# Gated FNet and attention mix: the last 22 units with whole products, two projection chains sooner, and maxima turned one section later

## The chip, the cores and the metric

The kernel runs on one core of a Trainium2 chip. The metric is the device time of one execution in microseconds (us). The times of before are three runs; one further execution was profiled, and the page and the trace come from it.

## The reference

The input x has 2048 rows of 512 columns. Two branches are mixed by a gate that is computed from x, one number for each row.

```
def _A_ref(x, dft_seq_re, dft_seq_im, dft_hid_re, dft_hid_im):
    a = einsum("bsd,ed->bse", x, dft_hid_re)
    b = einsum("bsd,ed->bse", x, dft_hid_im)
    return einsum("ts,bse->bte", dft_seq_re, a) - einsum("ts,bse->bte", dft_seq_im, b)

def _B_ref(x, wqkv, wo):            # H = 32 heads of 16 columns, S = 2048
    qkv = (x @ wqkv) ...            # split into q, k, v by head
    p = softmax(q @ k.T * 16 ** -0.5)
    return (p @ v, heads side by side) @ wo

g = sigmoid((x * gate_w).sum(-1, keepdims=True))
return g * _A_ref(...) + (1 - g) * _B_ref(...)
```

Everything is float32. The kernel keeps that accuracy by splitting a matrix into a high part and a remainder, and by taking three products (high-high, high-remainder, remainder-high) for one.

## The kernel before

The work has three stages. In the first (up to line 276) q, k, v and the transform along the hidden axis are computed with whole matmuls (128 rows of the array). In the second, the attention of 32 heads runs together with the transform along the sequence. In the third, the attention's output is divided by its sums, projected with `wo`, gated and written.

**Units.** Heads are taken in pairs; head 0 of a pair uses rows 0 to 63 of the TensorE array and head 1 rows 64 to 127, so that two matmuls of half height run at the same time. A pair has 32 units, and 16 pairs make 512 units. A unit is one block of 128 keys against 1024 queries (half `hf` of the queries). `scores(u, qb, h)` (line 554) makes a block of 128 x 512 scores in a bank of `psS` (three banks) and ScalarE takes the exponential of it into the tile `pt`; a unit has four such blocks. `pv(u)` (line 566) multiplies the four blocks with v, on four column groups of the array, into the bank `acc` ("the values of a unit"). After the sixteenth unit of a half `acc` is copied and stored.

**Maxima.** Softmax needs the largest score of each query ahead of time. `a_tile(i, h)` (line 196) computes a block of scores the other way round into a bank of `psA` (three banks), and VectorE takes the maximum along it into `mx`. Whenever the 64 blocks of one pair and half are done, VectorE reduces them to `nm`, and `(p, hf)` goes into the list `deferred`. `m_rows(p, hf)` (line 211) turns these maxima with a transpose on TensorE, copies them with two VectorE operations, and SyncE (SP) issues four DMAs that put them into two rows of `qs`; the scores of that pair and half take them in by their matmul (50 rows instead of 48). The maxima run ahead of the scores by `LEAD` blocks for each head, which are made in stage 1 among the whole matmuls (line 253).

**Products.** Next to the scores TensorE has a second stream of matmuls: first those of the sequence transform (`dft`, 32 chains of 48 products), then the projections (`proj(hf, cts, pools)`, chains of three products for each of the column tiles `cts`). A `Chain` accumulates in one bank (`psD`, or `psA` where `pools` names it). A product has 128 rows. In a section it is issued as two halves of 64 rows, one in each of two consecutive segments, so that a half product on one half of the array stands beside a score or a maxima block on the other half.

**Order.** TensorE, VectorE, ScalarE and SP each work through one queue in the order in which the program issues; the order is written by hand. A `segment` (line 712) handles two units and follows a pattern: a small letter is a slot with a half product and a score (`s`) or maxima (`a`) block of the other head; two letters are a slot with a block of each head; `|` stands for the values of one unit. FULL has 16 slots and 16 products, THIN 14 slots and up to 12 products. The two halves of a product must not accumulate into the bank at the same time. So the first product of a segment waits for the engine that used the last block of the segment before (`last_user`, line 725). At the end of a segment `run_deferred` issues the transposes of maxima that came due.

From unit 482 on the loop at the end (line 766) uses `weave` instead: nine products a section, first their halves on rows 64 to 127 and then their halves on rows 0 to 63, beside the scores of the two heads, with a TensorE drain (`turn`) ahead of each half; then the values of two units. Sections still have maxima blocks until unit 490. `start` sets which projection fills the sections. `plan` and `at(u, ...)` say ahead of which unit the other steps are issued: `sums` and `inverse` (the reciprocals of the softmax sums by way of DRAM), `block` and `last_block` (loading, multiplying and splitting the attention's output), `load_yg` and `load_w15`. `last_pair` (line 494) finishes the last head pair after the last values.

Of the kernel before, what the change touches and what calls it, by code (L numbers as in the profile page):

```python
# [9 lines left out]
F32 = mybir.dt.float32  # L10
# [5 lines left out]
P = 128  # L16
# [5 lines left out]
KT = D // P  # L22
NT = S // P
UNITS = NP * 32
LEAD = 42
RAW = 6
PSUM = bass.MemoryType.PSUM
DRAM = bass.MemoryType.DRAM
# [3 lines left out]
def mix_kernel(ctx: ExitStack, tc: tile.TileContext, xa_t, xa, wqkv, w_hid, w_seq, wo, gate_w, out):  # L32
# [191 lines left out]
    def run_deferred():  # L224
        while deferred:
            m_rows(*deferred.pop(0))
# [14 lines left out]
    for s in range(NT):  # L241
        ab[s] = t = xab[s // 4][:, s % 4]
        if s + 2 < NT:
            xgs[s + 2] = staged(xa[s + 2])
        xg = xgs.pop(s)
        pss = []
        for c in range(3):
            ps = psS.tile([P, 512], F32, name="s")
            pss.append(ps)
            for kt in range(KT):  # L250
                k = slice(kt * P, (kt + 1) * P)
                mm3(ps, t[:, 0, k], t[:, 1, k], wch[:, c, kt], wcl[:, c, kt], kt == 0, kt == KT - 1)
            for _ in range(2 if c == 1 and s % 4 == 0 else 1):
                if s >= 3 and a_next < LEAD:
                    a_tile(a_next, 0)
                    a_tile(a_next, 1)
                    a_next += 1
                    if a_next % 32 >= 4:
                        run_deferred()
            if c == 0:  # L260
                pv = ps.rearrange("p (r h d) -> p r h d", h=2, d=DH)
                nc.scalar.copy(vt[:, s, :, 0:16], pv[:, :, 0])
                nc.vector.tensor_copy(vt[:, s, :, 17:33], pv[:, :, 1])
        hi_lo(t[:, 0], t[:, 1], pss[1])
# [286 lines left out]

    pts = {}

    def scores(u, qb, h):
        p, r = divmod(u, 32)
        hf, kt = divmod(r, 16)
        q0 = hf * 1024 + qb * 512
        if u not in pts:
            pts[u] = work.tile([P, 4, 512], F32, name="pt", bufs=4)
        spare = a_next >= NP * 64 and qb and u < 500  # L560
        ps = psA.tile([P, 512], F32, name="a") if spare else psS.tile([P, 512], F32, name="s")
        rr = slice(64 * h, 64 * h + 50)
        nc.tensor.matmul(ps, ks[p % 2][rr, kt * P:(kt + 1) * P], qs[p % 2][rr, q0:q0 + 512], start=True, stop=True)  # L563
        return nc.scalar.activation(pts[u][:, 2 * qb + h], ps, AF.Exp, bias=0.0, scale=DH ** -0.5)  # L564
# [27 lines left out]

    def issue(x, half, stop=True):
        chain, st, mv, after, last = x
        i = chain.mm(st, mv, half, last and stop)
        if stop and after:
            after()
        return i

    def turn():  # L600

        nc.tensor.drain()

    def pump(gen, n):
        for x in take(gen, n):
            issue(x, None)

    def drain(gen):
        while xs := take(gen, 9):
            for x in xs:  # L610
                issue(x, None)

    def weave(q, ds):

        m = len(q[0]) - 1
        n = min(len(ds), m)
        if ds:
            turn()
        for i in range(n):
            q[0][i]()  # L620
            issue(ds[i], 1, False)
        for x in ds[n:]:
            issue(x, 1, False)
        for i in range(n, m + 1):
            q[0][i]()
            q[1][i - n]()
        rest = q[1][m + 1 - n:]
        if ds:
            turn()
        for i, x in enumerate(ds):  # L630
            issue(x, 0)
            if i < len(rest):
                rest[i]()

    fill = iter(())
    plan = {2: [gate]}

    def at(u, f, *args):
        plan.setdefault(u, []).append(partial(f, *args))
# [9 lines left out]
                    for step, du in enumerate((16, 20, 22)):  # L649
                        at(last + du + 8 * half, block, step, hf, ct, half)  # L650

    def start(gen, n, whole=True):
        nonlocal fill, rate
        drain(fill)
        fill, rate = gen, (n, whole)

    one, more = [(psD, "d")], [(psD, "d"), (psA, "a"), (psA, "a")]
    at(482, start, proj(0, (0, 1, 2), one), 9)
    at(482, load_yg, 0, range(8))
    for step, u in enumerate((490, 494, 496)):  # L660
        at(u, last_block, step, 1, 3, nc.gpsimd)
    at(500, start, proj(1, (3,), more), 9, False)
    for step, u in enumerate((500, 502, 504)):
        at(u, last_block, step, 0, 4, nc.vector)
    at(506, start, proj(0, (3,), more), 9, False)
    at(500, load_w15)
    rate = (7, True)
    lead = a_next

    def ahead(k):  # L670
        return min(lead + 4 * k, NP * 64)

    def queue(k, h):

        q = []
        for i in range(4):
            q.append(partial(scores, 2 * k + i // 2, i % 2, h))
            if ahead(k) + i < NP * 64:
                q.append(partial(a_tile, ahead(k) + i, h))
        return q  # L680

    def run_plan(k):
        for f in plan.get(2 * k, []) + plan.get(2 * k + 1, []):
            f()
        if k % 16 == 0 and k // 16 + 1 < NP:
            load_stacks(k // 16 + 1)

# [2 lines left out]

    FULL = "a s a s a s s a s a s a s a s a | |"
    THIN = "aS s s a a s a | a s a a s s sA |"

    def stream(h):

# [4 lines left out]

    streams = [stream(h) for h in range(2)]

    def score(kind, h):
        x = next(streams[h][kind == "a"], None)
        if x:
            last_user[0] = (a_tile if kind == "a" else scores)(*x)

    last_user = [None]  # L710

    def segment(k, pattern, half, ds, stop):

        before = last_user[0]
        ds = iter(ds)
        u = 2 * k
        for slot in pattern.split():
            if slot == "|":
                pv(u)
                u += 1  # L720
                continue
            if len(slot) == 1:
                x = next(ds, None)
                i = x and issue(x, half, stop)
                if i and before is not None:
                    tc.add_manual_dep(
                        i.ins, before.ins.name,
                        mybir.DependencyInfo(mybir.DependencyClass.Sync, mybir.DependencyReason.DATA))
                    before = None
            score(slot[0], 1 - half)  # L730
            if len(slot) == 2:
                score(slot[1].lower(), half)
        run_deferred()

    def pairs():

        seq = dft()
        for i in range(2 * NT):
            for _ in range(4 if i % 2 else 3):
                yield THIN if i % 2 else FULL, take(seq, 12 if i % 2 else 16)  # L740
        seq = proj(1, (0, 1, 2), one)
        for i in range(8):
            yield THIN, take(seq, 9)

    run_plan(0)
    for i in range(4):
        for kind in "sa":
            for h in range(2):
                score(kind, h)
    pv(0)  # L750
    pv(1)
    for i in range(4):
        score("s", 0)
        score("a", 0)
    last_user[0] = None
    k = 1
    for pattern, ds in pairs():
        for half in range(2):
            run_plan(k)
            a_next = ahead(k)  # L760
            segment(k, pattern, half, ds, half == 1)
            k += 1
    for f in queue(k, 1):
        f()
    a_next = ahead(k + 1)
    for k in range(k, UNITS // 2):
        run_plan(k)
        if 2 * k in pts:
            continue
        q = [queue(k, 0), queue(k, 1)]  # L770
        a_next = ahead(k)
        weave(q, take(fill, *rate))
        pv(2 * k - 2)
        pv(2 * k - 1)
        run_deferred()
    pv(UNITS - 2)
    pv(UNITS - 1, evac=False)
    last_pair(fill)


# [34 lines left out]
```

## Time and profile before

| what | value |
|---|---|
| three runs, median (lowest to highest) | 1835.68 us (1835.26 to 1836.51) |
| the profiled execution, its own time | 1838.79 us |
| span of the profiled execution | 1837.0 us |
| TensorE matmul busy (PE) | 1803.5 us, 98% of the span |
| VectorE busy (DVE) | 1424.6 us, 78% |
| ScalarE busy (ACT) | 1164.2 us, 63% |
| GpSimd busy (POOL) | 306.5 us, 17% |
| mean DMA rate | 90 GB/s |

The page names engines by short names: PE is TensorE (PEld its weight loads), DVE is VectorE, ACT is ScalarE, POOL is GpSimd, SP is SyncE, which issues the DMAs. In a line of the timeline the columns are start (us from the beginning of the span), duration (us), engine, line of the kernel, operation, output tile and inputs, shapes and the number of instructions; a bracket gives the idle time ahead and what ended it. In a line of the window table the columns are the window, its length, the busy time (and instructions) of PE, PEld, DVE, ACT and POOL, the granted TensorE clock (1.00 is full), the share of the DMA engines and GB/s. The ends of matmuls are modelled; their starts are what the steps are read from.

### The profile page before, as it was taken

To read this page: it belongs to the slowest core of one execution; us is meant where nothing else is said; L and a number is where in the kernel's file an instruction comes from. 1 tells how busy PE (TensorE), PEld (TensorE's weight loads), DVE (VectorE), ACT (ScalarE), POOL (GpSimd) and SP (SyncE) were. 2 spreads that over 40 slices of the span, in tenths; PEclk is the share of its full clock that TensorE was granted. 3 is DMA by queue.
4 is the path that set the end of the run, shared out by engine and by line. 5 is a ranking of instruction groups with operands and counts; after the bars stand their busy time and mean duration, and the time that the engine had idled before them with its cause. 6 is when DMAs were issued, how large, how long until landed. Compare 5 with 4: busy or idle time off the path is not lost.

```text
span 1837.0 us, 32546 instructions
## 1 busy us (share of the span) xinstructions
PE 1803.5 (98%) x12672; PEld 1034.7 (56%) x12672; DVE 1424.6 (78%) x2375; ACT 1164.2 (63%) x2240; POOL 306.5 (17%) x317
## 2 busy tenths in 40 slices
PE   8999999999999999999999999999999999999998
PEld 7876665555555545555555555554655455544554
DVE  5236668888888888888888888888888888888824
ACT  5311126777777777767676677767676777777664
POOL 1210011111212123121112222221112221100000
PEclk9999989999999999999999999999999999999999
DMA  8783233131414153414271434223231524360212
GB/s 283 256 194 106 69 97 60 39 67 36 76 36 70 37 111 94 81 36 70 89 211 49 76 100 100 58 53 64 63 66 49 110 89 87 116 184 7 71 37 92
DMA packets 77994, 164.71 MB, mean 90 GB/s; under 512 B 14592, under 2 KB 15616, under 8 KB 74000
## 3 DMA queue, kind: packets, MB, share of 16 engines
q1 hardware_dynamic: 77584, 162.56, 35.1%
q8 instruction: 100, 1.64, 0.4%
q14 instruction: 54, 0.44, 0.1%
q0 software_dynamic: 256, 0.07, 0.0%
HBM read 107.47 MB, written 54.52 MB: 88 GB/s over the span
## 4 chain that ended last, share of the span: by engine, by line
PE 94%; DVE 4%; issue 1%; ACT 1%; DMA 0%; DVEq 0%; SPq 0%; ACTq 0%
PE d L316 34%; PE acc L572 26%; PE a L201 12%; PE s L563 8%; PE s L78 4%; PE s L79 3%; PE s L80 3%; DVE mx L203 2%; PE a L78 1%; PE a L79 1%; PE a L80 1%; PE a L316 1%; DVE yp L456 1%; DVE rc L397 0%; PE a L213 0%
## 5 line engine op out<-in xcount | busy, mean ns | idle before, releaser
L203 DVE TENSOR_REDUCE mx<-a 128x1 f32<-128x512 f32 x2048 | 1280.9, 683 | 261.3 <-PE a L201 208.9
L564 ACT ACTIVATE pt<-s 128x512 f32<-128x512 f32 x2032 | 1060.3, 612 | 447.2 <-PE s L563 385.3
L201 PE MATMUL a<-ks,qs 48*128 48x512 f32 x2048 | 809.8, 428 | 5.4 <-DVE mx L203 5.4
L563 PE MATMUL s<-qs,ks 50*128 50x512 f32 x2032 | 739.8, 418 | 3.7 <-DVE xab L75 1.8
L316 PE MATMUL d<-xab,ch 64*128 64x512 f32 x2048 | 671.5, 405 | 8.5 <-DVE mx L203 6.6
L572 PE MATMUL acc<-pt,vt 128*17 128x512 f32 x4096 | 537.6, 598 | 0.0
L316 PEld LDWEIGHTS d<-xab,ch 64*128 64x128 f32 x2048 | 358.4, 185 | 203.1 <-issue 118.1
L201 PEld LDWEIGHTS a<-ks,qs 48*128 48x128 f32 x2048 | 373.7, 186 | 160.4 <-DVE mx L203 120.9
L563 PEld LDWEIGHTS s<-qs,ks 50*128 50x128 f32 x2032 | 365.7, 186 | 73.9 <-ACT pt L564 35.2
L316 PE MATMUL d<-xab,cl 64*128 64x512 f32 x1024 | 406.0, 396 | 0.0
L295 POOL CAST ch<-craw 128x512 fp32r<-128x512 f32 x128 | 78.2, 611 | 1132.8 <-PE s L563 678.6
L316 PEld LDWEIGHTS d<-xab,cl 64*128 64x128 f32 x1024 | 189.1, 185 | 42.1 <-DVE mx L203 23.8
L572 PEld LDWEIGHTS acc<-pt,vt 128*17 128x17 f32 x4096 | 87.3, 96 | 198.4 <-issue 187.0
L296 POOL TENSOR_TENSOR cl<-craw,ch 128x512 fp32r<-128x512 f32 x128 | 164.1, 1282 | 10.2
L316 PE MATMUL d<-wo_hl,o_hl 64*128 64x512 f32 x288 | 78.7, 405 | 3.8 <-DVE mx L203 2.9
L78 PE MATMUL s<-wch,xab 128*128 128x512 f32 x192 | 79.9, 416 | 0.0
L80 PE MATMUL s<-wch,xab 128*128 128x512 f32 x192 | 76.0, 396 | 0.0
L79 PE MATMUL s<-wcl,xab 128*128 128x512 f32 x192 | 75.9, 395 | 0.0
L74 ACT CAST xab<-s 128x512 fp32r<-128x512 f32 x16 | 9.4, 585 | 97.6 <-PE s L79 97.6
L316 PEld LDWEIGHTS d<-wo_hl,o_hl 64*128 64x128 f32 x288 | 49.5, 184 | 30.2 <-issue 17.7
L78 PEld LDWEIGHTS s<-wch,xab 128*128 128x128 f32 x192 | 36.0, 188 | 16.1 <-issue 6.4
L75 DVE TENSOR_TENSOR hl<-s,hl 128x512 fp32r<-128x512 f32 x32 | 22.0, 686 | 27.1 <-ACT hl L74 27.1
(101 smaller groups left out, 693.3 us busy)
## 6 DMA issues: line engine op xcount, KB each, us to landing
craw<-w_seq SPq DMA_DIRECT2D x128, 256.0 KB
qk<-hl SPq DMA_DIRECT2D x32, 512.0 KB
qs<-qk SPq DMA_DIRECT2D x96, 128.0 KB
ks<-qk SPq DMA_DIRECT2D x96, 128.0 KB
b<-hl SPq DMA_DIRECT2D x16, 512.0 KB
xab<-b SPq DMA_DIRECT2D x16, 512.0 KB
o<-oe SPq DMA_DIRECT2D x62, 128.0 KB
oh<-nh SPq DMA_DIRECT2D x12, 512.0 KB
```

Source lines behind the costliest of these rows:

```text
L75: (lo_eng or nc.vector).tensor_tensor(lo, src, hi.bitcast(F32), ALU.subtract)
L78: nc.tensor.matmul(ps, sh, mh, start=first, stop=False)
L79: nc.tensor.matmul(ps, sh, ml, start=False, stop=False)
L80: nc.tensor.matmul(ps, sl, mh, start=False, stop=last)
L201: nc.tensor.matmul(ps, qs[p % 2][r, qt * P:(qt + 1) * P], ks[p % 2][r, kb * 512:(kb + 1) * 512], start=True, stop=True)
L203: user = nc.vector.tensor_reduce(mx[p % 2][:, h, qt, kb:kb + 1], ps, AX.X, ALU.max)
L295: nc.gpsimd.tensor_copy(h1, raw)
L296: nc.gpsimd.tensor_tensor(l1, raw, h1.bitcast(F32), ALU.subtract)
L316: i = nc.tensor.matmul(self.ps, st[r], mv[r], start=not self.begun, stop=stop)
L563: nc.tensor.matmul(ps, ks[p % 2][rr, kt * P:(kt + 1) * P], qs[p % 2][rr, q0:q0 + 512], start=True, stop=True)
L564: return nc.scalar.activation(pts[u][:, 2 * qb + h], ps, AF.Exp, bias=0.0, scale=DH ** -0.5)
L572: nc.tensor.matmul(acc[32 * j:32 * j + 17], vt[:, kt, p, 16 * h:16 * h + 17], pt[:, j], start=kt == 0, stop=kt == NT - 1)
```

## The change

- `LEAD` goes from 42 to 44: two more pairs of maxima blocks are made in stage 1, for which six instead of three insertions are doubled.
- Pairs and segments: after the eight pairs of segments with `proj(1, (0, 1, 2))` two more pairs take the first two chains of `proj(0, (0, 1, 2))`. All ten pairs use two new patterns (NINE) with 12 and 13 slots for nine products.
- Maxima are turned one segment after they are complete, behind the first values of that segment, instead of at the end of the segment in which they are complete.
- The wait of a segment's first product goes to the last `s` block behind the last product of the segment before, where there is one, instead of to the last block.
- Last 22 units (490 to 511): `weave` and its drains go. A section issues three pairs of scores (head 0 in a `psS` bank, head 1 in a `psA` bank), then nine or six products as whole matmuls of 128 rows, then the fourth pair, then the values of two units. The last twelve products are issued in `last_pair`.
- The steps of the last blocks are planned for units 488, 492, 496 (from 490, 494, 496) and 500, 504, 504 (from 500, 502, 504). The loads of the stacks go into the plan at the same units as before.

```
-LEAD = 42
+LEAD = 44
...
-            for _ in range(2 if c == 1 and s % 4 == 0 else 1):
+            for _ in range(2 if c == 1 and s % 2 == 0 else 1):
...
-    def scores(u, qb, h):
+    def scores(u, qb, h, other=False):
...
-        spare = a_next >= NP * 64 and qb and u < 500
-        ps = psA.tile([P, 512], F32, name="a") if spare else psS.tile([P, 512], F32, name="s")
+        ps = psA.tile([P, 512], F32, name="a") if other else psS.tile([P, 512], F32, name="s")
...
-    def turn():
-
-        nc.tensor.drain()
-
     def pump(gen, n):
-        for x in take(gen, n):
+        for x in take(gen, n, False):
             issue(x, None)
...
-    def weave(q, ds):
...
-    for step, u in enumerate((490, 494, 496)):
+    for step, u in enumerate((488, 492, 496)):
         at(u, last_block, step, 1, 3, nc.gpsimd)
...
-    for step, u in enumerate((500, 502, 504)):
+    for step, u in enumerate((500, 504, 504)):
         at(u, last_block, step, 0, 4, nc.vector)
...
     FULL = "a s a s a s s a s a s a s a s a | |"
     THIN = "aS s s a a s a | a s a a s s sA |"
+    NINE = "sA s s a a sA | a a s a s aS |", "aS a s s a aS | sA a s a s s sA |"
...
+    def segment(pattern, half, ds, stop):
+        nonlocal users
+        before, users = users, []
+        due, deferred[:] = deferred[:], []
         ds = iter(ds)
         for slot in pattern.split():
             if slot == "|":
-                pv(u)
-                u += 1
+                values()
+                while due:
+                    m_rows(*due.pop(0))
                 continue
             if len(slot) == 1:
                 x = next(ds, None)
+                if x:
+                    i = issue(x, half, stop)
+                    users = []
+                    if before:
+                        tc.add_manual_dep(
+                            i.ins, dict(before).get("s", before[0][1]).ins.name,
...
-        run_deferred()
...
-        seq = proj(1, (0, 1, 2), one)
-        for i in range(8):
-            yield THIN, take(seq, 9)
+        for seq, n in ((proj(1, (0, 1, 2), one), 8), (first, 2)):
+            for i in range(n):
+                yield NINE, take(seq, 9)
...
+    run_plan(valued)
+    for i in range(4):
+        score("s", 1)
+    run_deferred()
+    pump(first, 9)
+    third = proj(1, (3,), more)
+    last = proj(0, (3,), more)
+    whole = {492: (first, 9), 494: (first, 9), 496: (first, 9), 498: (first, 9), 500: (first, 9), 502: (third, 9),
+             504: (third, 9), 506: (third, 6), 508: (last, 6), 510: (last, 6)}
+    for u in range(valued + 2, UNITS, 2):
+        run_plan(u)
+        for i in range(4):
+            if i == 3:
+                pump(*whole[u])
+            for h in range(2):
+                scores(u + i // 2, i % 2, h, h == 1)
+        values()
+        values()
     pv(UNITS - 2)
     pv(UNITS - 1, evac=False)
-    last_pair(fill)
+    last_pair(last)
```

`values()` issues `pv` for the next unit in turn, and `one` and `more` are `[psD]` and `[psD, psA, psA]`, the banks that the chains take in turn.

More of the change, by code (lines that the diff above doesn't have):

```diff
@@ L611, in drain @@
                 issue(x, None)
-    def weave(q, ds):
[L615 to L635, printed above, removed]
     plan = {2: [gate]}
@@ L650, in mix_kernel, with run_plan @@
                         at(last + du + 8 * half, block, step, hf, ct, half)
[L652 to L655, printed above, removed]
+    for p in range(1, NP):
+        at(32 * (p - 1), load_stacks, p)
     one, more = [(psD, "d")], [(psD, "d"), (psA, "a"), (psA, "a")]
-    at(482, start, proj(0, (0, 1, 2), one), 9)
     at(482, load_yg, 0, range(8))
-    for step, u in enumerate((490, 494, 496)):
+    for step, u in enumerate((488, 492, 496)):
         at(u, last_block, step, 1, 3, nc.gpsimd)
-    at(500, start, proj(1, (3,), more), 9, False)
-    for step, u in enumerate((500, 502, 504)):
+    for step, u in enumerate((500, 504, 504)):
         at(u, last_block, step, 0, 4, nc.vector)
-    at(506, start, proj(0, (3,), more), 9, False)
     at(500, load_w15)
-    rate = (7, True)
     lead = a_next
[L670 to L686, printed above, removed]
+    def run_plan(u):
+        for v in sorted(v for v in plan if v <= u + 1):
+            for f in plan.pop(v):
+                f()
     FULL = "a s a s a s s a s a s a s a s a | |"
     THIN = "aS s s a a s a | a s a a s s sA |"
+    NINE = "sA s s a a sA | a a s a s aS |", "aS a s s a aS | sA a s a s s sA |"
     def stream(h):
@@ L703, in mix_kernel @@
     streams = [stream(h) for h in range(2)]
+    users, valued = [], 0
     def score(kind, h):
@@ L707, in score, with values @@
         if x:
[L708 to L714, printed above, removed]
+            users.append((kind, (a_tile if kind == "a" else scores)(*x)))
+    def values():
+        nonlocal valued
+        pv(valued)
+        valued += 1
+    def segment(pattern, half, ds, stop):
+        nonlocal users
+        before, users = users, []
+        due, deferred[:] = deferred[:], []
         ds = iter(ds)
-        u = 2 * k
         for slot in pattern.split():
             if slot == "|":
-                pv(u)
-                u += 1
+                values()
+                while due:
+                    m_rows(*due.pop(0))
                 continue
@@ L723, in segment @@
                 x = next(ds, None)
[L724 to L729, printed above, removed]
+                if x:
[4 more added lines that the diff above has]
+                            i.ins, dict(before).get("s", before[0][1]).ins.name,
+                            mybir.DependencyInfo(mybir.DependencyClass.Sync, mybir.DependencyReason.DATA))
+                        before = None
             score(slot[0], 1 - half)
@@ L739, in pairs @@
             for _ in range(4 if i % 2 else 3):
-                yield THIN if i % 2 else FULL, take(seq, 12 if i % 2 else 16)
-        seq = proj(1, (0, 1, 2), one)
-        for i in range(8):
-            yield THIN, take(seq, 9)
+                yield ((THIN,) * 2, take(seq, 12)) if i % 2 else ((FULL,) * 2, take(seq, 16))
+        for seq, n in ((proj(1, (0, 1, 2), one), 8), (first, 2)):
+            for i in range(n):
+                yield NINE, take(seq, 9)
+    first = proj(0, (0, 1, 2), one)
     run_plan(0)
@@ L749, in mix_kernel @@
                 score(kind, h)
-    pv(0)
-    pv(1)
+    values()
+    values()
     for i in range(4):
@@ L754, in mix_kernel @@
         score("a", 0)
-    last_user[0] = None
-    k = 1
-    for pattern, ds in pairs():
+    users = []
+    for patterns, ds in pairs():
         for half in range(2):
[L759 to L775, printed above, removed]
+            run_plan(valued)
+            segment(patterns[half], half, ds, half == 1)
+    run_plan(valued)
+    for i in range(4):
+        score("s", 1)
+    run_deferred()
+    assert not any(a_left.values())
+    pump(first, 9)
[10 more added lines that the diff above has]
+                scores(u + i // 2, i % 2, h, h == 1)
+        values()
+        values()
     pv(UNITS - 2)
     pv(UNITS - 1, evac=False)
-    last_pair(fill)
+    last_pair(last)
 def kernel(A_x, A_dft_seq_re, A_dft_seq_im, A_dft_hid_re, A_dft_hid_im, B_x, B_wqkv, B_wo, gate_w):
```

## The prediction

> **What bounds it now.** I read the page first: busy times and the chain that ended last.
>
> ```profile
> PE 1803.5 (98%) x12672; PEld 1034.7 (56%) x12672; DVE 1424.6 (78%) x2375; ACT 1164.2 (63%) x2240; POOL 306.5 (17%) x317
> ...
> PE 94%; DVE 4%; issue 1%; ACT 1%; DMA 0%; DVEq 0%; SPq 0%; ACTq 0%
> ```
>
> TensorE is the bound in every stage, so time is saved by taking slots off TensorE, as long as VectorE (78%) does not take over. Then the window table, cut where the order of work changes: the 16 THIN segments with nine products (units 450 to 481), the first hand-over and weave sections, the last ten weave sections, the end.
>
> ```profile
> 1624.76:1722.36 97.60, 94.67 (x662) 45.48 (x658) 86.79 (x143) 69.51 (x131) 1.84 (x2) 1.00 0.21 49
> 1722.36:1751.44 29.08, 27.65 (x193) 16.46 (x189) 23.89 (x40) 19.21 (x37) 2.39 (x1) 1.00 0.31 101
> 1751.44:1820.60 69.16, 66.64 (x411) 35.24 (x410) 18.71 (x26) 43.21 (x85) 2.53 (x2) 1.00 0.17 48
> 1820.60:1837.00 16.40, 10.72 (x65) 5.27 (x64) 8.74 (x25) 2.27 (x10) 0.00 (x0) 0.79 0.43 161
> ```
>
> A THIN segment with nine products takes 97.60/16 = 6.10 us, a weave section 6.9, and in the weave sections VectorE (18.71 of 69.16) and ScalarE (43.21) are half idle. One weave section in the timeline of TensorE:
>
> ```profile
> 1760.66 0.49 PE L563 MATMUL s<-qs,ks 50*128 50x512 f32 x1
> ...
> 1762.84 0.39 PE L563 MATMUL s<-qs,ks 50*128 50x512 f32 x1
> 1763.33 0.49 PE L316 MATMUL d<-wo_hl,o_hl 64*128 64x512 f32 x1
> ...
> 1764.12 1.55 PE L316 MATMUL d<-wo_hl,o_hl 64*128 64x512 f32 x6
> 1765.60 1.91 PE L572 MATMUL acc<-pt,vt 128*17 128x512 f32 x16
> 1767.76 0.47 PE L563 MATMUL s<-qs,ks 50*128 50x512 f32 x1 [0.25 <-issue]
> ```
>
> A slot (one matmul, or two on the two row halves) is 0.232 us: six in 1.55 with 0.39 for the last. The section is 7.1 us: 19 slots (nine half products, nine more, one pair of scores alone) = 4.4, two units of values = 1.75, the rest edges and two drains (0.49 instead of 0.23 at 1762.84).
>
> **Tail sections, units 492 to 511.** Afterwards a section has four pairs and nine whole products: 13 slots = 3.02 instead of 4.4. Two values with their edges and no drain: a FULL segment is 5.95 between values in the timeline, less 16 slots leaves 2.24. Switching from pairs to whole rows and back has a row in stage 1, where a pair stands among whole matmuls:
>
> ```profile
> 133.49 0.40 PE L80 MATMUL s<-wch,xab 128*128 128x512 f32 x1
> 133.82 0.50 PE L201 MATMUL a<-ks,qs 48*128 48x512 f32 x2
> 134.25 0.50 PE L78 MATMUL s<-wch,xab 128*128 128x512 f32 x1
> 134.58 0.40 PE L79 MATMUL s<-wcl,xab 128*128 128x512 f32 x1
> ...
> 137.24 0.73 PE L201 MATMUL a<-ks,qs 48*128 48x512 f32 x3
> 138.53 0.50 PE L201 MATMUL a<-ks,qs 48*128 48x512 f32 x1 [0.55 <-DVE mx L203]
> 138.96 0.50 PE L78 MATMUL s<-wch,xab 128*128 128x512 f32 x1
> ```
>
> From 133.49 to 134.58 are 1.09 for three slots (0.70): 0.40 for both switches. So 5.66 by this sum; walking the gaps one by one (0.52, 0.33, 0.23, 0.43, 0.34, 1.63, 0.33, 0.34, 1.32) gives 5.47. I take 5.55, and 4.85 for a section with six products. The Trainium skill, "TensorEngine Tiling (Array Packing)", Key Properties, says that a change of tiling mode drains TensorE, which speaks against mixing whole and halved matmuls; the trace agrees, at 0.40 us. With free switches the ten sections would sum to 4 us less; the page has no price.
>
> ScalarE has eight exponentials a section; a row of eight below takes 4.03, under 4.85. The sixth score bank is free when pair 3 comes, since the products stand in between. In sections 502 to 510 the products share the three psA banks with head 1's scores: a product waits for the exponential of pair 0 or 1, about 0.35 in 502 and 504, 0.1 to 0.2 later (between 0 and 1 each). In 504 the cast of the last raw block queues ahead of the exponentials on ScalarE (1.08), behind a multiply on VectorE that needs a DMA. In before that multiply started at 1789.81 and the values of unit 495 ended at 1774.4: 15.4 us. The new place is three sections later, some 16 us: cover just enough, 0.6 more taken for the cast, 2 to 4 if the DMA is late. Sum: 5 x 5.55 + 5.9 + 6.5 + 5.05 + 2 x 4.95 = 55.1. The hand-over ahead of it (four single scores, one transpose of maxima, nine whole products) is 1.6 + 0.3 + 2.4 = 4.3.
>
> **Units 450 to 489, pattern NINE.** Twelve and thirteen slots instead of fourteen: 12.5 x 0.232 = 2.90, and two separate values at 0.87 + 0.41 of edges = 2.56; 5.46. (The same sum for THIN gives 5.81; it measures 5.88 with twelve products.) With nine it measures 6.10 because the first product of the next half waits for the last maximum, which stands behind the evacuation of the chain:
>
> ```profile
> 1636.92 0.50 PE L563 MATMUL s<-qs,ks 50*128 50x512 f32 x1
> 1637.78 0.49 PE L316 MATMUL d<-wo_hl,o_hl 64*128 64x512 f32 x1 [0.36 <-DVE mx L203]
> ...
> 1733.29 4.95 DVE L203 TENSOR_REDUCE mx<-a 128x1 f32<-128x512 f32 x8 [0.96 <-PE a L201]
> ...
> 1796.70 4.03 ACT L564 ACTIVATE pt<-s 128x512 f32<-128x512 f32 x8 [1.82 <-PE d L316]
> ```
>
> That wait goes, as it is tied to an exponential (0.50 each) instead. What is late next is VectorE: per pair of segments 16 maxima at 0.62, an evacuation 0.75, 0.2 of row work = 10.87, 5.43 a segment. TensorE and VectorE are level. I take 5.55; floor 5.34, ceiling the present 6.10. Twenty segments: 111.0.
>
> From 1624.76 (0.98 behind the start of unit 449's values, where the first such segment begins) to the end of the last values (1824.05, the last pass at 1823.63 plus 0.42) are 199.3 us. Afterwards 111.0 + 4.3 + 55.1 + 1.75 = 172.2: **-27.1**.
>
> **The end.** Twelve whole products (four chains) move behind the last values. TensorE is idle there, but four evacuations at 0.66 enter VectorE's queue between the reciprocals and the last eight evacuations, and those 21% of the chain's last 22 us end last: **+2.4** (1.5 to 3).
>
> **Stage 1.** LEAD 44 needs six double insertions of maxima instead of three, and one single less. A single costs 0.64, a double 1.91 (the second pair waits for a psA bank, row 138.53): 3 x 1.27 = +3.8. The pair dropped at 257.6 no longer stands ahead of VectorE's subtraction that the second score waits for (idle 1.75 at 260.06): -1.1. **+2.7.**
>
> **The middle.** Turning maxima is moved: the transposes go one section later, behind its first values. In before each costs 0.21 and none waits for VectorE beyond the end of the values. In THIN that stays; in FULL it now splits two values: 13 times 0.25, between 0 and 0.5 (nearest: edges of 0.41 around a single value): +3.2. SP issues its four DMAs 0.9 to 2.9 us sooner; nothing queues behind them. The other change is the wait of the first product, "s" instead of the last user:
>
> ```profile
> 608.18 1.09 ACT L564 ACTIVATE pt<-s 128x512 f32<-128x512 f32 x2
> ...
> 608.82 0.47 PE L316 MATMUL d<-xab,ch 64*128 64x512 f32 x1 [0.23 <-ACT pt L564]
> ...
> 1201.41 0.47 PE L316 MATMUL d<-xab,ch 64*128 64x512 f32 x1 [0.89 <-DVE mx L203]
> ```
>
> Inside a chain both users end within 0.1 us of each other: nothing. Where a chain of the first matrix ends, ScalarE evacuates it and the exponential ends at 609.27, so the product moves from 608.82 to 609.40: 8 x 0.58 = +4.6. Where one of the second ends, VectorE evacuates and the product need not wait for the maximum: 4 x 0.65 + 3 x 0.77 = -4.9. The plan's earlier loads at 488 and 492 move on SP and POOL alone, 15 us ahead of use: nothing. **+2.9.**
>
> Sum: -27.1 + 2.4 + 2.7 + 2.9 = **-19.1**. The profiled execution took 1838.79 us (span 1837.0 and 1.8 around it), 3.1 above the median of 1835.68; taken off the median, **1816.5 us**.
>
> **Rivals.**
> VectorE takes over in NINE: three psA banks do not bridge the values, segments stay near 6.1. For: 5.43 of 5.55. Against: VectorE ran eight in a row without a gap. 20 x 0.55: 1827.5. Chance 0.15.
> The last block's DMA or the shared psA banks hold the tail: for, VectorE already waited 2.0 us for that DMA; against, 7 us of slack to its user. +4: 1820.5. Chance 0.10.
> The clock: after the 1.75 us without TensorE work at 260.06 the granted clock is 0.50 in windows of 5 us from 260 to 275 and 0.79 in the next, some 17 us; the change cuts that gap to about 1. If the clock stays, values and a segment run at full speed until VectorE's 20 maxima bind: -5.5, 1811. Against: the slots there stay 0.6 apart. Chance 0.10. The Trainium skill, "TensorE: Matmul & The Clock Gate", Why this matters for your kernels, puts the limit at idle gaps over some 3 us; by that rule not even the old gap should have cost the clock, and the trace disagrees.
> Slower: the rows of maxima reach qs too late, so that the scores of each of 30 groups wait. It decides from 19.1/30 = 0.64 us each; at 1 us, 1846.5. Against: they are issued sooner than before. Chance 0.05.
> The gain is not there, since the sections become bound by ScalarE's latency and stay near 6.9 and NINE near 6.1: 1835. Chance 0.04.
> My sum: 0.56.
>
> **Range.** 0.2% (3.7 us) is what can be told from no change. Low 1806: the VectorE floor in NINE (-4.2) and the clock rival. High 1828: the first rival. Left out are the last two. Faster 0.91, same 0.03, slower 0.06.
>
> **What would show it.** Values of one NINE segment to the next 5.4 to 5.7 apart; tail sections 5.4 to 5.7 and 4.7 to 5.0, without 0.49 gaps; at the ends of first-matrix chains the product released by an exponential about 0.6 later; VectorE without a gap longer than 1 us in the end. Wrong would be NINE over 5.9, a gap of 2 us in section 504, or scores waiting for DMA of the maxima.

## The result and the profile after

The changed kernel takes **1815.79 us** (median of 4 runs, 1815.06 to 1815.92), the kernel before 1836.10 us (median of 4, 1835.26 to 1839.22). The ratio is 0.9885, 95% interval 0.9868 to 0.9903, so it is faster by 1.0 to 1.3%. Forecast were 1816.5 us. The profiled execution took 1815.83 us, with a span of 1814.0. One of the executions below, the profiled one of best_lead44 (2349.89 us), ran at a granted clock of 0.65 throughout and is left out of that kernel's time.

The page of the changed kernel, busy times and the chain that ended last:

```profile
PE 1787.5 (99%) x12570; PEld 1020.6 (56%) x12570; DVE 1423.9 (78%) x2375; ACT 1160.5 (64%) x2240; POOL 306.5 (17%) x317
...
PE 96%; DVE 2%; ACT 1%; issue 0%; DMA 0%; POOL 0%; DVEq 0%; ACTq 0%; POOLq 0%
```

TensorE has 102 matmuls fewer and is still the bound: its part of the chain went from 94 to 96%, VectorE's from 4 to 2%. VectorE's own work is what it was.

The window table of the changed kernel: nineteen and a half NINE segments, up to the end of the values of unit 488; then the last half segment, the hand-over and section 492 up to its values; from there to the values of unit 510, which are the two values of section 492 and the nine sections 494 to 510; the end from the start of these last values. The columns are busy time of PE, PEld, DVE, ACT and POOL, then the granted clock, the DMA share and GB/s.

```profile
1624.21:1735.74 111.53, 110.74 (x802) 52.13 (x798) 104.78 (x173) 81.42 (x158) 4.23 (x3) 1.00 0.26 69
1735.74:1746.46 10.72, 10.50 (x56) 6.06 (x52) 3.90 (x8) 7.70 (x16) 0.00 (x0) 1.00 0.01 2
1746.46:1797.25 50.79, 50.00 (x307) 22.43 (x309) 15.76 (x21) 40.51 (x78) 2.55 (x2) 1.00 0.19 49
1797.25:1814.00 16.75, 11.58 (x64) 6.65 (x56) 10.42 (x28) 1.71 (x8) 0.00 (x0) 0.80 0.54 204
```

TensorE's own idle time is 0.8 us in each of the two long stretches: what is left there is the length of TensorE's list and the edges between its items. VectorE is busy for 104.78 of the 111.53 us of the NINE segments (94%; 89% before), so it is near the bound and, but for one place shown further down, not on it.

A tail section in the timeline of TensorE (start, duration, engine, line, operation):

```profile
1751.89 1.91 PE L571 MATMUL acc<-pt,vt 128*17 128x512 f32 x16
1753.73 0.49 PE L562 MATMUL s<-qs,ks 50*128 50x512 f32 x1
1754.30 0.39 PE L562 MATMUL s<-qs,ks 50*128 50x512 f32 x1
1754.63 2.33 PE L316 MATMUL d<-wo_hl,o_hl 128*128 128x512 f32 x9
1756.89 0.50 PE L562 MATMUL s<-qs,ks 50*128 50x512 f32 x1
1757.32 1.05 PE L571 MATMUL acc<-pt,vt 128*17 128x512 f32 x8
```

From values to values are 5.43 us: two values 1.84, three pairs 0.90, nine whole products 2.26 from 1754.63 to 1756.89, the last pair and the step to the values 0.43. Two pairs of changes between halves and whole rows are inside these numbers, without any wait.

Two places of a NINE segment, also from the timeline of TensorE:

```profile
1633.78 0.39 PE L316 MATMUL d<-wo_hl,o_hl 64*128 64x512 f32 x1
1634.20 0.50 PE L201 MATMUL a<-ks,qs 48*128 48x512 f32 x1
1634.63 1.05 PE L571 MATMUL acc<-pt,vt 128*17 128x512 f32 x8
...
1635.61 0.50 PE L562 MATMUL s<-qs,ks 50*128 50x512 f32 x1
1635.96 0.40 PE L316 MATMUL d<-wo_hl,o_hl 64*128 64x512 f32 x1
```

The product that opens the half (1635.96) stands 0.35 us behind the first score and carries no wait; before it stood 0.86 behind and waited 0.36 for a maximum. The slot ahead of the values (1634.20, the last letters "sA" or "aS") is 0.42 from the slot before it and 0.43 from the values.

### The profile page after: what moved, and what is told of

Read it like the earlier page. It is cut to its first block, busy times and chain, and to the rows that moved or that the text cites. A ratio compares the mean times of both kernels' runs of the same rounds, so it can differ in the third digit from the quotient of the medians.

```text
span 1814.0 us, 32329 instructions
## 1 busy us (share of the span) xinstructions
PE 1787.5 (99%) x12570; PEld 1020.6 (56%) x12570; DVE 1423.9 (78%) x2375; ACT 1160.5 (64%) x2240; POOL 306.5 (17%) x317
## 4 chain that ended last, share of the span: by engine, by line
PE 96%; DVE 2%; ACT 1%; issue 0%; DMA 0%; POOL 0%; DVEq 0%; ACTq 0%; POOLq 0%
PE d L316 34%; PE acc L571 27%; PE a L201 12%; PE s L562 9%; PE s L78 4%; PE s L79 3%; PE s L80 3%; DVE mx L203 1%; PE a L79 1%; PE a L78 1%; PE a L80 1%; ACT pt L563 1%; PE a L316 0%; PE a L213 0%; DVE y L348 0%
## 5 line engine op out<-in xcount | busy, mean ns | idle before, releaser
L563 ACT ACTIVATE pt<-s 128x512 f32<-128x512 f32 x2008 | 1046.5, 612 | 423.8 <-PE s L562 367.9
L562 PE MATMUL s<-qs,ks 50*128 50x512 f32 x2008 | 730.1, 418 | 1.1 <-DVE xab L75 0.7
L201 PEld LDWEIGHTS a<-ks,qs 48*128 48x128 f32 x2048 | 369.9, 185 | 168.6 <-DVE mx L203 134.8
L562 PEld LDWEIGHTS s<-qs,ks 50*128 50x128 f32 x2008 | 359.8, 185 | 87.1 <-ACT pt L563 46.0
L316 PE MATMUL d<-wo_hl,o_hl 64*128 64x512 f32 (+1 forms) x234 | 63.2, 398 | 0.0
L316 PEld LDWEIGHTS d<-wo_hl,o_hl 64*128 64x128 f32 (+1 forms) x234 | 42.1, 186 | 13.0 <-issue 7.9
```

The source lines that it names most:

```text
L201: nc.tensor.matmul(ps, qs[p % 2][r, qt * P:(qt + 1) * P], ks[p % 2][r, kb * 512:(kb + 1) * 512], start=True, stop=True)
L316: i = nc.tensor.matmul(self.ps, st[r], mv[r], start=not self.begun, stop=stop)
```

## The experiments

Each edit is against the changed kernel. All times are medians of at least four runs; the kernel before ran beside them on the same chip, with 1837.82, 1837.32 and 1836.32 us in the three groups. The groups ran on three different chips, and the changed kernel itself beside the last of them only (the control), so a difference of 1 to 2 us to its 1815.79 is not told apart by the times; there the segments and sections in the traces decide. By "middle" are meant the stretches from the values of unit 2 to those of 252 (first matrix: 748.6 us before, 752.6 after) and from 252 to 450 (600.5 and 594.7).

**Control: the changed kernel again.**

> The changed kernel itself, unedited, beside the two on the same chip: 1815 to 1816.5; its half clock after stage 1 lasts anything from 3.4 to 17 us, in whole steps of 3.4.

Measured: 1814.86 us (1814.50 to 1815.02), ratio 0.9882 (0.9867 to 0.9897), a little under what was expected. The half clock lasts 3.4 us.

### The wait of the first product

**e1_last_user.** The product waits for the last user again, as before.

```
-  i.ins, dict(before).get("s", before[0][1]).ins.name,
+  i.ins, before[-1][1].ins.name,
```

> The changed kernel, but the first product of a segment waits again for the user of the last block of the segment before. Theory (the wait is what the first product starts on): in the middle the 8 gaps at the ends of first-matrix chains fall from 1.42 to 0.82 us and the 7 at the ends of second-matrix chains rise from 0.88 or 1.00 to 1.48 or 1.60, net about -0.6; in the ten NINE pairs the product that follows a chain's end waits about 0.5 us more, +5. Sum +4, about 1820. Rival (VectorE sets the pace of NINE by its queue, the wait does not matter): NINE stays at 5.72 us a segment, about 1815.

Measured: 1819.32 us (1816.80 to 1820.08), ratio 0.9900 (0.9885 to 0.9915). The middle moves as said: 747.8 (-4.8) and 599.3 (+4.6). In the NINE segments the wait comes back, but smaller than the 0.36 of before (timeline of this kernel):

```profile
1638.08 0.50 PE L316 MATMUL d<-wo_hl,o_hl 64*128 64x512 f32 x1 [0.16 <-DVE mx L203]
```

They take 5.87 instead of 5.72: over the twenty the kind of wait is worth 2.8 us of NINE's gain, little more than half of what was expected. That the total still came out near the 1820 expected is luck: in this execution the half clock behind stage 1 lasts 13.7 us, and the values of unit 2 start 2.0 us later (280.78 instead of 278.78). The one run with a granted clock of 0.997 took 1816.80 us.

**e2_first_user.** The product waits for the first user, whatever its kind.

```
-  i.ins, dict(before).get("s", before[0][1]).ins.name,
+  i.ins, before[0][1].ins.name,
```

> The changed kernel, but the first product of a segment waits for the user of the block that was issued beside the last product (the first in the list, not the last exponential). Theory: at the ends of first-matrix chains the exponential waited for ends 0.5 us sooner, so the 8 gaps of 1.42 fall to about 0.9, -4; the second-matrix ends stay (there the evacuation is last), NINE stays. About 1811.8. Rival (the bank's evacuation on ScalarE is what holds these products): the gaps stay at 1.42, 1815.8.

Measured: 1811.30 us (1810.46 to 1812.82), ratio 0.9860 (0.9843 to 0.9876). The first-matrix stretch takes 748.5 (-4.1); the second (594.7) and the NINE segments (5.72) stay. At the end of a chain of the first matrix the timelines show why, first in the changed kernel, then in this one:

```profile
611.07 1.08 ACT L563 ACTIVATE pt<-s 128x512 f32<-128x512 f32 x2
...
612.30 0.47 PE L316 MATMUL d<-xab,ch 64*128 64x512 f32 x1 [0.82 <-ACT pt L563]
```

```profile
609.83 0.47 PE L316 MATMUL d<-xab,ch 64*128 64x512 f32 x1 [0.33 <-ACT pt L563]
```

Behind ScalarE's evacuation stand two exponentials (x2 in 1.08 us). The changed kernel's product starts 0.15 us behind the end of the second of them, since "the score" is the last one of the list; here it starts 0.5 to 0.6 us sooner, behind the first. So the choice of "the score" gains at the chain ends of the second matrix and in NINE and loses at those of the first; "the first user" loses next to nothing there (0.33 of idle time, where before had 0.23).

### The pattern NINE and the tail sections

**e3_thin.** The NINE segments with the old pattern, but the new wait.

```
-  yield NINE, take(seq, 9)
+  yield (THIN,) * 2, take(seq, 9)
```

> The changed kernel with the pattern THIN (14 slots) in place of NINE (12 and 13) for the ten pairs with nine products. Theory A (slots set the pace): 1.5 slots of 0.232 more in each of 20 segments, less the longer edge at NINE's two-letter slots (0.09 at each value): from 5.72 to about 5.85 us a segment, +2.6, about 1818.4. Theory B (the slots alone, no edge cost): 6.07 a segment, +7, 1823. Theory C (VectorE sets the pace): no change, 1815.8.

Measured: 1820.02 us (1818.76 to 1821.28), ratio 0.9906 (0.9891 to 0.9921). A segment takes 5.94 instead of 5.72, and the twenty 4.1 us more: between what A and B expected, against C. Of the step from 6.10 to 5.72 the pattern makes 0.22, and the rest, 0.16, goes with the wait.

**e5_drains.** A drain before and behind the whole products of each tail section.

```
+  nc.tensor.drain()
   pump(*whole[u])
+  nc.tensor.drain()
```

> The changed kernel with a TensorE drain ahead of and behind the whole products of each of the ten tail sections. Theory (a switch between pairs and whole matmuls already empties the array, 0.40 us a round trip, but an explicit drain adds the restart): 0.25 us each as the drain in the middle of a weave section cost, +5, about 1820.5. Rival (the switch is a full drain by itself): no change, 1815.8.

Measured: 1818.96 us (1817.40 to 1819.52), ratio 0.9900 (0.9886 to 0.9915). The sections 494 to 500 take 5.84, +0.41; the five later ones only 0.10 to 0.17 more than without drains. In this kernel's timeline the steps into and out of the products are 0.53 and 0.58, where the changed kernel has 0.33 and 0.40:

```profile
1760.91 0.39 PE L562 MATMUL s<-qs,ks 50*128 50x512 f32 x1
1761.44 2.33 PE L316 MATMUL d<-wo_hl,o_hl 128*128 128x512 f32 x9
1763.88 0.49 PE L562 MATMUL s<-qs,ks 50*128 50x512 f32 x1
```

In these sections a drain is 0.2 us on top of a change of tiling that goes on without it.

**e6_halves.** The sections' products in halves, woven with the scores as before, with the two drains and the score banks of before; the units and the chains of the change are kept.

```
-  for i in range(4): ... pump(*whole[u]) ... scores(u + i // 2, i % 2, h, h == 1)
+  weave([[partial(scores, u + i // 2, i % 2, h, i % 2 == 1 and u < 500) ...
```

> The changed kernel with the ten tail sections issued as before: half products with two drains, no whole ones (the scores on the banks that before used). Theory (slots set the pace of the tail): seven sections with nine products have 19 slots instead of 13 (+1.39) and 0.25 more for drains, three with six have 13 instead of 10 (+0.70) and 0.25: +14 in all, sections of 7.0 and 6.0 us, about 1830. Rival (ScalarE's eight exponentials and the shared banks set the pace): under +7, sections below 6.2.

Measured: 1829.82 us (1829.06 to 1832.03), ratio 0.9964 (0.9953 to 0.9975). The sections with nine products are back at 7.0 to 7.2 us, those with six at 6.1, as the count of slots has it: 14 of the change's 20 us hang on issuing whole products, without drains. How much of the 14 goes with the drains and the score banks was not run alone; the rival (under 7 us) is out.

### Maxima turned later, and LEAD

**e4_lead42.** LEAD 42 as before, everything else as changed.

```
-LEAD = 44
+LEAD = 42
-  for _ in range(2 if c == 1 and s % 2 == 0 else 1):
+  for _ in range(2 if c == 1 and s % 4 == 0 else 1):
   ...
   score("s", 1)
+  if i < 2:
+      score("a", 1)
```

> The changed kernel with LEAD 42 and the three double insertions of before; the two blocks of head 1 that are left over come after the tenth pair, beside the single scores. Theory (what stage 1 pays for LEAD 44 is given back by the shorter stretch at half clock): the first values start 2.9 us sooner, at 265.0, the half clock lasts 17 us again instead of 6.8, the second section's values are within 1 us of the changed kernel's 278.8; +0.5 at the end; 1815 to 1816.5. Rival (the clock is a matter of chance): half clock 6.8 us again, 1813.

Measured: **1845.0 us** (1844.01 to 1846.78), ratio 1.0043 (1.0028 to 1.0058). Every theory missed it by more than 28 us. The timelines of this kernel show where they went, TensorE first, then SP's DMA queue between its second and third row:

```profile
306.27 0.28 PE L213 MATMUL a<-ident,nm 128*16 128x128 f32 x1
307.46 0.49 PE L201 MATMUL a<-ks,qs 48*128 48x512 f32 x1
310.58 0.62 PE L562 MATMUL s<-qs,ks 50*128 50x512 f32 x2 [2.63 <-DMA qs<-mt]
```

```profile
307.92 2.76 SPq L220 DMA_DIRECT2D qs<-mt  x4
```

The group of maxima is turned at 306.27, SP issues the DMAs of its four rows from 307.92 to 310.68, and the next score needs rows of its head: TensorE stands for 2.63 us. The same wait recurs, 20.6 us in 13 places. Five times the clock goes to half 0.8 to 1.6 us behind the end of one, for 3.41 us (waits of 2.63, 2.27, 1.60, 3.06 and 2.62 us); behind the other eight, of 0.27 to 1.19 us, it stays. The half clock can cost at most half of 5 x 3.41, 8.5 us, so that waits and clock together make most of the 29 us lost. In the windows of this kernel around the first the granted clock is 0.86, 0.50, 0.75 and 1.00:

```profile
310.58:312.00 1.42, 1.42 (x11) 1.37 (x12) 0.18 (x1) 0.91 (x2) 0.00 (x0) 0.86 0.03 6
312.00:314.00 2.00, 2.00 (x14) 0.48 (x11) 1.80 (x3) 1.26 (x3) 0.00 (x0) 0.50 0.00 0
314.00:316.00 2.00, 2.00 (x18) 1.01 (x12) 0.53 (x1) 0.32 (x1) 0.00 (x0) 0.75 0.00 0
316.00:318.00 2.00, 2.00 (x18) 0.63 (x14) 1.95 (x4) 1.87 (x5) 0.00 (x0) 1.00 0.00 0
```

Turning later costs the rows one section of their head start, and two more in LEAD are what buys it back. From the transpose to the first values of its group pass at least 13.9 us in before, 15.1 in the changed kernel, 13.3 in e8_lead42_end and 10.5 in this one. This is the prediction's slower rival, kept away by one constant.

**e7_rows_end.** LEAD 44, but the maxima turned at the end of the segment as before.

```
-  due, deferred[:] = deferred[:], []
   ...
-  while due:
-      m_rows(*due.pop(0))
   ...
+  run_deferred()
```

> The changed kernel (LEAD 44), but maxima are turned at the end of the segment in which they are complete, as before. Theory: in THIN and NINE they are complete with the last slot, so the transpose waits for the last maximum and its reduction on VectorE, about 0.55 us more at some 17 places, and FULL saves 0.1 at 13: +8, about 1824. Rival (the transpose needs nothing that is late): 1814.5.

Measured: 1822.32 us (1821.65 to 1823.69), ratio 0.9921 (0.9906 to 0.9936). With LEAD 44 the group is complete later in its segment, so a transpose at the segment's end comes too soon; it waits for VectorE's reduction, in 18 places and for 9.5 us in all:

```profile
347.06 0.22 DVE L207 TENSOR_REDUCE nm<-mx 128x16 f32<-128x64 f32 x1
347.33 0.28 PE L213 MATMUL a<-ident,nm 128*16 128x128 f32 x1 [0.39 <-DVE nm L207]
```

**e8_lead42_end.** Both undone: LEAD 42 and the turn at the segment's end (the edits of the last two together).

> The changed kernel with LEAD 42 (three double insertions) and the maxima turned at the end of the segment, both as before. Theory (LEAD 42 alone lost 29 us because the rows then reach qs one section too late and the scores wait for them; with the earlier turn no score waits): no stretch of half clock after the start, stage 1 is 2.9 us shorter, the middle has the six gaps of before back (+3.4): about 1815 to 1816, so that the pair of edits is worth nothing here. Rival (LEAD 42 costs by its number of blocks alone, wherever they are turned): about 1845.

Measured: 1814.30 us (1814.15 to 1816.75), ratio 0.9880 (0.9865 to 0.9894): the same as the control. The pair of edits is worth nothing; each alone loses 7 and 30 us. It is a balance of small parts: stage 1 is 3.0 us shorter (values of unit 0 at 264.85 instead of 267.89), and the middle 1.3 longer (753.1 and 595.6). For the second, the timeline of this kernel, VectorE and TensorE:

```profile
641.30 0.28 DVE L215 CAST mt<-a 16x128 fp32r<-16x128 f32 x1 [0.85 <-PE a L213]
641.61 0.28 DVE L216 TENSOR_TENSOR mt<-a,mt 16x128 fp32r<-16x128 f32 x1
641.82 1.11 DVE L397 RECIPROCAL rc<-rc 64x64 f32<-64x64 f32 x2
642.96 3.68 DVE L203 TENSOR_REDUCE mx<-a 128x1 f32<-128x512 f32 x6
643.71 0.50 PE L201 MATMUL a<-ks,qs 48*128 48x512 f32 x1 [0.39 <-DVE mx L203]
```

The copies of the maxima and two reciprocals stand in front of the next maxima, and the pair behind them finds no free psA bank. In the changed kernel the copies begin beside the second values:

```profile
641.64 1.05 PE L571 MATMUL acc<-pt,vt 128*17 128x512 f32 x8
641.75 0.28 DVE L215 CAST mt<-a 16x128 fp32r<-16x128 f32 x1
```

There the first pair of the next segment has no such wait. Before has it in six places, 0.39 to 0.63 us each, and e8_lead42_end in six again.

### A version that beats both

**best_lead44** and **best_lead42.** Three edits together, once on the changed kernel and once on e8_lead42_end (there with `s % 4`): the first-user wait; in stage 1 the second pair of maxima put into the middle of the chain, not beside the first; and the last chain on two banks in place of three, so that its products do not share psA's with the scores as often.

```
+  if kt != KT - 1 and not (kt == 1 and c == 1 and s % 2 == 0):
+      continue
-  for _ in range(2 if c == 1 and s % 2 == 0 else 1):
-  dict(before).get("s", before[0][1]).ins.name
+  before[0][1].ins.name
-  last = proj(0, (3,), more)
+  last = proj(0, (3,), more[:2])
```

> Three edits to the changed kernel together: the first product waits for the user of the block beside the last product (-4.2, measured alone); in stage 1 the six doubled insertions are pulled apart, the second pair standing in the middle of the chain, where it costs 0.64 instead of 1.27 us (-3.8); the last chains take the banks d, a in turn, so that no section begins its products on a psA bank (-0.6, section 510). If the terms add: 1807.5. Rival (what stage 1 saves is lost again at VectorE or in the half clock behind it): 1811.

> The same three edits on LEAD 42 with the maxima turned at the end of the segment: from 1814.3, -4.2 for the wait, -1.9 for three insertions pulled apart, -0.6 for the banks: 1807.6. If the six gaps of about 0.5 us, where the reciprocals stand ahead of the copies of maxima, are what LEAD 44 takes away, this one stays within 1 us of the other.

Measured: 1807.2 us (1806.28 to 1808.04), ratio 0.9840 (0.9827 to 0.9854), and 1807.35 us (1807.08 to 1808.66), ratio 0.9843 (0.9829 to 0.9856): 7.5 to 7.7 us under the control of the same group and 29 under before. The terms add up to within 1 us, and the two leads are worth the same again. The profile of best_lead42 shows the terms: the values of unit 0 start at 263.18 (264.85 in e8_lead42_end), the first-matrix stretch takes 749.1, and section 510 takes 4.98 instead of 5.59, while all other tail sections stay. Only the first of the three edits was run alone.

## Why the prediction was right, step by step

The forecast of 1816.5 us was 0.7 over the median. Its mechanism holds: TensorE's list was cut, and VectorE did not take over. Its terms were not all of the right size, and several misses offset each other: that the total is only 0.7 off is in part luck.

**From unit 450 to the end of the last values: forecast -27.1, measured -24.5** (174.8 us against 199.3). By its parts:
- *NINE*, taken at 5.55: measured 5.72 up to the values of unit 488, and 114.7 us for all twenty: 3.7 us too little. It isn't the ceiling of VectorE: the opening product carries no wait. Against the counted sum of 5.46 one edge is longer: the step from the two-letter slot to the values is 0.43, not 0.33, four times in a pair of segments, which is 0.18 a segment or a little more. And three of the ten pairs of segments are longer, 0.08 a segment on average: two in which rows are turned, by 0.4, and one, by 0.8, in which VectorE does hold TensorE up, as two reciprocals stand among the maxima (VectorE, then TensorE):

```profile
1721.18 1.12 DVE L397 RECIPROCAL rc<-rc 48x64 f32<-48x64 f32 x2
1723.07 0.49 PE L201 MATMUL a<-ks,qs 48*128 48x512 f32 x1 [0.70 <-DVE mx L203]
```

The row of 0.36 for the old wait was the right row for a wrong share: e1 gives it 0.14 a segment, e3 the pattern 0.22.
- *Sections 492 to 500*, taken at 5.55: 5.43 each from 494 on. The walk by gaps (5.47) was the better of the two sums. The hand-over ahead of them, taken at 4.3, took 3.9.
- *502 and 504*, taken at 5.9 and 6.5: 5.90 and 5.89; *506 and 508*, taken at 5.05 and 4.95: 4.98 each. The raw block's multiply came directly behind the last evacuation and waited for no DMA, and the cast hid:

```profile
1774.34 1.22 DVE L442 TENSOR_TENSOR o_raw<-o_raw 128x1024 f32<-128x1024 f32 x1
1775.58 1.05 ACT L74 CAST o_l<-o_raw 128x1024 fp32r<-128x1024 f32 x1 [0.41 <-DVE o_raw L442]
```

- *510*, taken at 4.95: 5.59. The shared psA banks, put at 0.1 to 0.2 there, cost 0.77:

```profile
1793.50 0.96 PE L316 MATMUL a<-wo_hl,o_l 128*128 128x512 f32 x3 [0.77 <-ACT pt L563]
```

**The end: forecast +2.4, measured +2.1** (16.75 us from the last values' start, 14.68 before). VectorE has the four evacuations more, as said; it now opens with one and runs through without a gap to the last:

```profile
1800.08 1.45 DVE L456 SCALAR_TENSOR_TENSOR yp_ks<-a,omg,yp_ks 128x512 f32<-128x512 f32 x2 [4.13 <-PE a L316]
...
1809.27 1.40 DVE L456 SCALAR_TENSOR_TENSOR yp<-a,omg,yp 128x512 f32<-128x512 f32 x2
```

**Stage 1: forecast +2.7, measured +2.9** at the values of unit 0, and only +0.6 at those of unit 2. The clock rival came in by half: after the shorter gaps (0.74 and 0.49 us instead of 1.75) the granted clock is 0.50 for 6.8 us, not 17.1. The windows of the changed kernel:

```profile
260.00:265.00 5.00, 3.78 (x17) 2.12 (x16) 2.91 (x7) 3.07 (x6) 0.00 (x0) 0.95 0.14 55
265.00:270.00 5.00, 5.00 (x21) 2.18 (x25) 3.91 (x7) 2.36 (x5) 1.50 (x2) 0.50 0.63 212
270.00:275.00 5.00, 5.00 (x27) 2.48 (x21) 2.79 (x6) 2.87 (x7) 4.04 (x5) 0.87 0.40 105
```

How long it stays there isn't set by the gaps: the control has the same two (0.74 and 0.49) and 3.4 us, e1 and e7 have 0.74 and 0.47 or 0.48 and 13.7 us, and e4 has one gap of 1.75, as before, and 6.8. So these 2.3 us (+2.9 at unit 0 less +0.6 at unit 2) differ between executions and can't be put down to the change.

**The middle: forecast +2.9, measured -1.7** (1347.3 against 1349.0, units 2 to 450). This is the step with the wrong sign. The two parts from the wait were right: +0.60 at each chain end of the first matrix (forecast +0.58) and -0.60 at those of the second (forecast -0.65 and -0.77); the latter in the changed kernel, where the product is released by the evacuation and not by a maximum:

```profile
1202.99 0.74 DVE L348 SCALAR_TENSOR_TENSOR y<-d,ng,yr 128x512 f32<-128x512 f32 x1
1203.88 0.47 PE L316 MATMUL d<-xab,ch 64*128 64x512 f32 x1 [0.29 <-DVE y L348]
```

Too high was the price of a turn in FULL: 0.32 between the values less 0.21 at the segment's end is 0.1, not 0.25. Not seen were the six gaps where copies and reciprocals follow each other on VectorE: 3.3 us of waits that the later turn takes away. e8, where they come back, shows it.

**How the sum stands.** The measured parts, -24.5, +2.1, +0.6 and -1.7, come to -23.5, less 0.6 that is counted twice at unit 450: the 23.0 us by which the profiled spans differ. The forecast sum was -19.1, so between the profiled executions it was 3.9 too small, 2.3 of them the clock's. The medians differ by 20.3 only, since the profiled execution of before lay 3.1 over its median of that time; the sum was taken off the median, and that is why the total came out closer than the terms did. The runs show what such 3 us are: of 26 runs of the kernel before in the three groups the 13 with a granted clock of 0.992 to 0.994 took 1837.50 to 1839.27 us, the 13 with 0.995 or 0.996 took 1835.18 to 1837.14. The profiled execution had 0.993; all eight runs of the changed kernel have 0.996 or 0.997.

**The rivals.** VectorE in NINE: excluded as what sets the pace by the opening product without a wait; it held TensorE up once, for 0.70 us, and 0.17 of the rival's 0.55 a segment appeared, most of it by another way. The last block's DMA: did not wait; the shared banks cost 0.6 in one section. The sections' latency: 5.43 with 1.6% of TensorE's time idle. The late rows: real, in e4, at 1.6 us in each of 13 places and the clock besides, and absent at LEAD 44.

**The two rules.** The trace agrees with the Trainium skill, "TensorEngine Tiling (Array Packing)", Key Properties, that a change of tiling mode drains TensorE, in so far as it costs time: 0.40 us a round trip in stage 1's row. That the array empties fully is not shown; e5's drains cost more than the change alone. With nine whole products behind it, the change pays: a section is some 1.6 us shorter than in e6. The limit of idle time that the Trainium skill gives in "TensorE: Matmul & The Clock Gate", Why this matters for your kernels, some 3 us, does not agree with these runs: the clock went to half after 1.75 us without TensorE work in before, after gaps of 0.74 and 0.49 us in the changed kernel and after single waits from 1.60 us on in e4, where those up to 1.19 us left it alone. Length alone is not the rule, since two gaps of under 0.75 did it behind stage 1. All changes of the clock in one of these traces lie whole multiples of 3.41 us apart (in e4 the drops at 260.41 and 311.61, 15 steps), so where a gap falls on this grid may count as well; no run here isolates it.

## What to carry to other kernels

Where two forms of tiling alternate, price the change of form from a row that shows it and set it against the slots that it saves; a drain around it is another 0.2 us, where nothing else waits, that nothing needed. A manual wait should name the event that is done first among those that are enough, and the place of each chain end decides which that is. When a step is moved behind another, count the head start of everything that it issues: here one section of it was worth 30 us, and a constant far off in stage 1 held it. Before a time is compared to 2 us, look at the granted clock of the runs: here it alone moved the same kernel by that much.

## What was not expected of the hardware

The stretches at half clock behind stage 1 were 3.4, 6.8, 13.7 or 17.1 us long, which are 1, 2, 4 and 5 times 3.41 us, over twelve profiles; why an execution gets one or five is open. SP takes 2.76 us to issue four small row DMAs, half a segment, and in e4 the score that needed them started 4.3 us behind the transpose (306.27 to 310.58). And two edits that lose 7 and 30 us when one of them is undone are worth nothing together, which no run with one alone could have told.
